# Where eight stage 1 groups stand among the taps of a long convolution, and which engine empties their tiles

## The chip, the cores and the metric

The kernel runs on one core of one Trainium2 chip. The metric is the device time in microseconds of one execution; the time of a kernel is the median over its runs. A profile is one execution recorded instruction by instruction, and its span is counted from the first to the last recorded instruction.

## The reference, cut to what matters

```
k_shift[t, d] = sum over j of k[t - j, d] * shift_k[d, j]        # ks = 4
kv   = k_shift * v                                                # S = 2048, D = 512
y    = irfft2( rfft2(pad kv to 2S) * rfft2(pad ssm_k to 2S) )[:S] + kv * ssm_D
h    = x + layernorm(x) * y                                       # x = A_q
out  = h + relu(layernorm(h) @ w1) @ w2                           # w1 512 x 1376
```

Everything is bf16 at the edges. The convolution is along the 2048 tokens, one filter (a row of `ssm_k`) for each of the 512 channels.

## The kernel before, in words

The long convolution is done as a two-step Fourier transform with matmuls. Both operands, the filter `ssm_k` and the product `kv`, go through the same three steps: `to_rows` transposes them with TensorE into a flat layout (`kfl` for the filter, `xfl` for kv), `stage1` does the short first transform, and `stage2` the second one. After the filter's spectrum and the signal's spectrum are multiplied, two inverse steps and a two-layer MLP follow.

**What loads.** SyncE issues nine loads in the order of line 119: chunk 0 of k, the whole of `ssm_k`, chunk 0 of v, and then chunks 1, 2 and 3 of k and of v in turn. A chunk is 512 tokens. The k and v chunks are DMA transposes (lines 125 and 127), so that channels come to lie on partitions: `kT` holds k, `vTs[c]` holds chunk c of v.

**The taps.** `taps(u)` (line 271) makes one of 16 units. `u` is split into a chunk `c = u // 4` and a block of 128 channels `rg = u % 4`. Four matmuls of 128x128 by 512 columns accumulate the four shifted products in one PSUM tile `pkv` (line 275). `times_v(u, ps)` (line 282) multiplies that tile by `vTs[c]` on VectorE and writes it to `kvx`. Units 0 to 3 run before the transposes of the filter. Units 4 to 15 run inside the loop of line 311.

**The stage 1 groups.** `group_k(gb)` (line 286) is group gb of eight for the filter. It takes four PSUM tiles, and for each of 8 columns and two halves of the table it issues four small matmuls (a load of 32x128 weights and a matmul with 64 columns, line 248): 64 pairs of load and matmul, 128 instructions, in about 0.6 us. Then each of the four tiles is copied into `a1k` by ScalarE or VectorE: the string given to `stage1` has one letter a tile, A for ScalarE (`copy`, line 235) and D for VectorE (line 237), read by `engs[(4 * gb + rg) % len(engs)]`.

**What sets the order.** The schedule is written by hand: every engine runs its instructions in the order of the program text. All PSUM tiles of this part have one tag (`ps`) in a pool of 8 banks; a new tile takes the bank that was given back longest ago, and its first matmul waits for the copy that empties this bank.

**What comes after.** `to_rows` for kv (line 321) transposes `kvx` in eight steps of 8 transposes (line 221, tiles `pst`), each emptied by VectorE (line 225) or ScalarE (line 230). The first of its transposes reads all channels and all chunks, so it waits for the last `times_v` (u = 15). Then `spectrum_k` (stage 2 of the filter, lines 263, 265, 335 and 336) alternates with the stage 1 groups of kv, which have the same line 248 but read `xfl`.

I number the filter's groups gk0 to gk7 and the units u4 to u15. In the kernel before, TensorE's order in the loop is: u4 u5 gk0, u6 gk1, u7 u8 gk2, u9 gk3, u10 u11 gk4, u12 gk5, u13 u14 gk6, u15 gk7. Each group's tiles go A, A, D, A.

Of the kernel before, what the change touches and what calls it, by code (L numbers as in the profile page):

```python
# [56 lines left out]
def kernel(  # L57
# [175 lines left out]
    def copy(eng, o, i):  # L233
        if eng == "A":
            nc.scalar.copy(out=o, in_=i)  # L235
        else:
            nc.vector.tensor_copy(out=o, in_=i)  # L237


    def stage1(gb, fl, a_out, engs, parts=1):  # L240
        n = 8 // parts
        for h in range(parts):
            pss = [psum.tile([P, n, 64], F32, tag="ps", name=f"ps1_{r}") for r in range(4)]
            for gi in range(n):
                for f, first in ((f1hi, True), (f1lo, False)):
                    for rg in range(4):
                        rows = slice(32 * rg, 32 * rg + 32)
                        nc.tensor.matmul(out=pss[rg][:, gi, :],  # L248
                                         lhsT=fl[rows, (8 * gb + n * h + gi) // 2, :, :, gi % 2].rearrange("p d n -> p (d n)"),
                                         rhs=f[rows, :], start=first, stop=not first, tile_position=(32 * rg, 0))  # L250
            for rg in range(4):
                copy(engs[(4 * gb + rg) % len(engs)], a_out(gb, 8 * rg + n * h, n),
                     pss[rg][:].rearrange("p g c -> p c g"))
# [17 lines left out]
    def taps(u):  # L271
        c, rg = divmod(u, DC)
        ps = psum.tile([P, CH], F32, tag="ps", name="pkv")
        for j in range(KS):
            nc.tensor.matmul(out=ps[:], lhsT=wdiag[:, rg, j, :], rhs=kT[:, rg, CH * c + 16 - j:CH * c + CH + 16 - j],  # L275
                             start=(j == 0), stop=(j == KS - 1))
        return u, ps

    def times_v(u, ps):
        c, rg = divmod(u, DC)  # L280
        split = "p (a h l) -> p a h l"
        nc.vector.tensor_tensor(out=kvx[:, :, rg, 8 * c:8 * c + 8, :].rearrange("p h a l -> p a h l"),  # L282
                                in0=ps[:].rearrange(split, h=16, l=4),
                                in1=vTs[c][:, rg, :].rearrange(split, h=16, l=4), op=ALU.mult)

    def group_k(gb):
        stage1(gb, kfl, lambda o, j, n: a1k[:, :, 32 * o + j:32 * o + j + n], "AADAAADA")

    first = [taps(u) for u in range(4)]
    warm_up(7)  # L290
# [1 line left out]
    kfl = early.tile([P, 32, 2, 64, 2], BF16, name="kfl")  # L292
# [15 lines left out]
    a1k = a1[:, 8 * 256:72 * 256].rearrange("p (c j) -> p c j", j=256)  # L308
    a1x = a1[:, 0:64 * 256].rearrange("p (o c j) -> p o c j", o=8, j=32)

    for gb in range(8):
        for u in ((4, 5), (6,), (7, 8), (9,), (10, 11), (12,), (13, 14), (15,))[gb]:
            times_v(*taps(u))
        group_k(gb)
    for pq in halves:
# [364 lines left out]
```

## Time and profile before

| what | value |
|---|---|
| median of 13 runs | 219.98 us (218.8 to 220.74) |
| the profiled execution's own time | 219.25 us |
| its span | 217.5 us |
| TensorE busy | 205.7 us, 95% of the span |
| VectorE busy | 147.4 us, 68% |
| ScalarE busy | 128.1 us, 59% |
| the loop of lines 311 to 314 on TensorE | 18.51 us (u4 starts) to 37.03 us (first transpose of kv) |
| matmul line 275, 128x512 | 380 ns each by the record, four in about 0.93 us |
| VectorE multiply by v, line 282 | 680 to 693 ns |
| VectorE copy of a stage 1 tile, line 237 | 686 ns |
| ScalarE copy of a stage 1 tile, line 235 | 595 ns |

How to read it: the span is some 1.75 us shorter than the execution's time, which has a start and an end around it. Durations of neighbours on one engine overlap a little: three ScalarE copies in a row take 1.56 us, six take 3.16 us, and VectorE starts a new tile every 0.60 us while each record is 0.69 us long. In the rows of the profile, "<-" behind an idle time names what ended it, and "issue" means that nothing which the profile shows was waited for. PEld is the loading of weights, which has its own row beside PE.

### The profile page before, as it was taken

What the parts mean: (1) busy time and instruction counts of PE and PEld (TensorE: products, weight loads), DVE (VectorE), ACT (ScalarE), POOL (GpSimd) and SP (SyncE); (2) the same over time, 40 slices, a digit from 0 to 9 for tenths busy, and PEclk for the clock granted to TensorE, in tenths of its full rate; (3) what the DMA queues carried; (4) which work ended last, traced back from release to release, by engine and by line L of the source; (5) the groups of instructions that cost most, each with busy time, mean ns of one, the idle gap of its engine ahead of it and who ended that gap; (6) DMA issues with size and microseconds to landing.
All of it is one profiled execution on the core that took longest, in us unless ns stands there. A gap on an engine that the chain in (4) does not pass through costs nothing.

```text
span 217.5 us, 7309 instructions
## 1 busy us (share of the span) xinstructions
PE 205.7 (95%) x3129; PEld 140.0 (64%) x3129; DVE 147.4 (68%) x303; ACT 128.1 (59%) x241; POOL 65.5 (30%) x99
## 2 busy tenths in 40 slices
PE   7979889999999999999987999999999999999993
PEld 2466446999989999889955687444444444444442
DVE  6977678899989998958967778743874267130032
ACT  2487857788878888868865699004740067106500
POOL 6049930000039999968000121210021002000000
PEclk9999999999999999999999799999999999999999
DMA  6999960000000000069960000422123110531012
GB/s 136 360 187 176 193 127 8 3 5 3 3 3 3 2 3 0 0 161 215 323 214 6 3 3 0 60 60 55 27 57 68 33 44 0 85 75 36 0 42 54
DMA packets 30383, 15.40 MB, mean 71 GB/s; under 512 B 25520, under 2 KB 29072, under 8 KB 30224
## 3 DMA queue, kind: packets, MB, share of 16 engines
q1 hardware_dynamic: 28992, 14.75, 29.8%
q8 instruction: 24, 0.39, 0.7%
q10 hardware_dynamic: 1360, 0.20, 0.6%
q14 instruction: 7, 0.06, 0.1%
HBM read 7.08 MB, written 2.10 MB: 42 GB/s over the span
## 4 chain that ended last, share of the span: by engine, by line
PE 77%; SPq 9%; DVE 6%; DMA 3%; ACT 2%; issue 2%; DVEq 0%
PE ps2m L595 18%; PE ps1m L583 16%; PE pz L509 10%; PE psy L385 7%; SPq L127 5%; PE psi L454 4%; PE ps2k L263 4%; PE u L263 4%; PE ps L248 4%; PE u L265 4%; SPq L125 3%; PE ps2k L265 3%; DMA vT<-in_A_v_dram 3%; PE pkv L275 3%; DVE bp L237 2%
## 5 line engine op out<-in xcount | busy, mean ns | idle before, releaser
L585 ACT ACTIVATE h1T<-ps1m 128x512 bf16<-128x512 f32 (+3 forms) x55 | 27.4, 514 | 21.2 <-PE ps1m L583 20.3
L583 PE MATMUL ps1m<-hlnT,w 128*128 128x512 bf16 (+3 forms) x220 | 39.6, 336 | 0.3
L595 PE MATMUL ps2m<-w,h1T 128*128 128x512 bf16 (+3 forms) x187 | 39.8, 367 | 0.0
L597 DVE TENSOR_TENSOR o<-ps2m,xh 128x512 bf16<-128x512 f32 (+1 forms) x17 | 11.1, 659 | 38.1 <-PE ps2m L595 37.6
L583 PEld LDWEIGHTS <-w 128*128 128x128 bf16 (+1 forms) x220 | 21.8, 100 | 17.6 <-issue 1.4
L595 PEld LDWEIGHTS <-h1T 128*128 128x128 bf16 (+1 forms) x187 | 17.6, 98 | 21.2 <-issue 3.1
L509 PE MATMUL pz<-bp,ecore 32*32 32x128 f32 x1024 | 23.2, 386 | 2.9 <-issue 2.3
L520 ACT CAST zt<-pz 128x512 bf16<-128x512 f32 x16 | 8.4, 593 | 29.5 <-PE pz L509 28.2
L235 ACT CAST a<-ps 128x512 fp32r<-128x512 f32 x40 | 21.1, 593 | 4.3 <-PE ps L248 4.3
L529 POOL TENSOR_SCALAR rstd<-mv 128x4 f32<-128x4 f32 (+1 forms) x7 | 1.6, 232 | 70.5 <-DVE mv L536 70.5
L509 PEld LDWEIGHTS pz<-bp,ecore 32*32 32x32 f32 x1024 | 14.4, 106 | 10.4 <-issue 6.8
L375 POOL TENSOR_TENSOR t<-usb,kf 128x320 fp32r<-128x320 f32 x22 | 19.5, 914 | 1.7 <-ACT usb L366 1.6
L375 DVE TENSOR_TENSOR t<-u,kf 128x704 fp32r<-128x704 f32 x22 | 18.5, 899 | 1.7 <-ACT usb L366 1.6
L235 ACT CAST kf<-psy 128x512 fp32r<-128x512 f32 x30 | 17.6, 644 | 1.8 <-PE psy L385 0.3
L534 DVE BATCH_NORM_STATS2 st<-xh 128x6 f32<-128x512 bf16 x28 | 17.4, 681 | 0.0
L237 DVE CAST a<-ps 128x512 fp32r<-128x512 f32 x24 | 15.8, 686 | 1.9 <-PE ps L248 1.9
L275 PE MATMUL pkv<-kT,wdiag 128*128 128x512 bf16 x64 | 15.6, 384 | 0.0
L454 PE MATMUL psi<-dre,kf 128*128 128x256 f32 x64 | 15.2, 284 | 0.2 <-ACT kf L235 0.2
L454 PE MATMUL psi<-dim,kf 128*128 128x256 f32 x64 | 15.1, 285 | 0.0
L213 POOL TENSOR_SCALAR c2n<-c2s 128x512 fp32r<-128x512 f32 x8 | 11.9, 1509 | 9.1 <-ACT c2s L181 9.1
L282 DVE TENSOR_TENSOR kvx<-pkv,vT 128x512 bf16<-128x512 f32 x16 | 10.7, 688 | 4.6 <-DMA vT<-in_A_v_dram 2.6
L336 ACT CAST kf<-ps2k 128x512 fp32r<-128x512 f32 x16 | 10.7, 666 | 3.1 <-PE ps2k L265 1.8
(123 smaller groups left out, 402.4 us busy)
## 6 DMA issues: line engine op xcount, KB each, us to landing
pre<-in_A_ssm_k_dram SPq DMA_DIRECT2D x1, 2048.0 KB, 10.5
out_dram<-o SPq DMA_DIRECT2D x58, 32.0 KB, 1.6
xh<-in_A_q_dram SPq DMA_DIRECT2D x4, 384.0 KB, 7.0
w<-in_B_w_dram SPq DMA_DIRECT2D x1, 1376.0 KB, 12.4
w<-in_B_w_dram SPq DMA_DIRECT2D x1, 1280.0 KB, 15.4
xh<-in_A_q_dram SPq DMA_DIRECT2D x4, 128.0 KB, 3.3
hlnT<-hln SPq DMA_TRANSPOSE x12, 2.4
w<-in_B_w_dram SPq DMA_DIRECT2D x1, 96.0 KB, 15.1
```

Of the source, the lines that this page charges most:

```text
L235: nc.scalar.copy(out=o, in_=i)
L237: nc.vector.tensor_copy(out=o, in_=i)
L263: nc.tensor.matmul(out=ps[:, kk, :], lhsT=w_re[:, k1, :], rhs=a_in(col(k1, 0)), start=True, stop=False, skip_group_check=True)
L265: nc.tensor.matmul(out=ps[:, kk, :], lhsT=w_im[:, k1, :], rhs=a_in(col(k1, 1)), start=False, stop=True, skip_group_check=True)
L275: nc.tensor.matmul(out=ps[:], lhsT=wdiag[:, rg, j, :], rhs=kT[:, rg, CH * c + 16 - j:CH * c + CH + 16 - j], start=(j == 0), stop=(j == KS ...
L375: eng.tensor_tensor(out=t[:, :, j, :], in0=in0.unsqueeze(1).to_broadcast([P, 2, n, 2]), in1=kfr[:, :, j, ks], op=ALU.mult)
L454: nc.tensor.matmul(out=ps, lhsT=kf[:, c, 4 * m:4 * m + 4, :].rearrange("p r k -> p (r k)"), rhs=(dre, dim)[c][:].rearrange("p a b -> p (a ...
L509: nc.tensor.matmul(out=pz[32 * a:32 * a + 32, r4, l4, :], lhsT=ecore[rows, rho, n2, :], rhs=rhs, start=(rho == 0), stop=(rho == 1), tile_p ...
L534: nc.vector.bn_stats(out=st[:, t % 4, :], in_=xh[:, t, :])
L583: nc.tensor.matmul(out=ps1[:fsz, :], lhsT=w1[:, c, fc * P:fc * P + fsz], rhs=hlnTs[sc][:, c, part], start=(c == 0), stop=(c == DC - 1))
L585: nc.scalar.activation(out=h1s[sc][:fsz, fc, part], in_=ps1[:fsz, :], func=ACT.Relu)
L595: nc.tensor.matmul(out=ps2[:], lhsT=h1s[sc][:ksz, fc, i * P:(i + 1) * P], rhs=w2[:ksz, fc, ds], start=(fc == 0), stop=(fc == NFC - 1))
```

## The change

Two lines change. The units of the taps are handed out differently over the eight groups, and the string of engines is written out for all 32 tiles.

```diff
     def group_k(gb):
-        stage1(gb, kfl, lambda o, j, n: a1k[:, :, 32 * o + j:32 * o + j + n], "AADAAADA")
+        stage1(gb, kfl, lambda o, j, n: a1k[:, :, 32 * o + j:32 * o + j + n], "AADAADADADADADADADADADADAAAAAAAA")
...
     for gb in range(8):
-        for u in ((4, 5), (6,), (7, 8), (9,), (10, 11), (12,), (13, 14), (15,))[gb]:
+        for u in ((4, 5), (6, 7), (), (), (8, 9), (10, 11), (12, 13), (14, 15))[gb]:
             times_v(*taps(u))
         group_k(gb)
```

TensorE's order in the loop becomes: u4 u5 gk0, u6 u7 gk1, gk2, gk3, u8 u9 gk4, u10 u11 gk5, u12 u13 gk6, u14 u15 gk7. So gk0 to gk3 stand ahead of u8, the first unit of the third chunk, and gk1, gk2 and gk3 stand in a row. The tiles go A, A, D, A in gk0, A, D, A, D in gk1 to gk5, and A, A, A, A in gk6 and gk7: VectorE has 11 of the 32 copies (8 before) and ScalarE 21 (24 before). TensorE's instructions are the same in number and kind. GpSimd's and SyncE's instructions and their order are unchanged.

## The prediction

> **What bounds the kernel now.** I read the page first, then the chain of waits, and then TensorE's and VectorE's timelines cut to 18 to 43 us, because both edits lie inside the loop that ends at 37.03 us.
>
> ```profile
> PE 205.7 (95%) x3129; PEld 140.0 (64%) x3129; DVE 147.4 (68%) x303; ACT 128.1 (59%) x241; POOL 65.5 (30%) x99
> ```
>
> TensorE is busy for 95% of the span, so what moves the time is mainly where it stands still. The chain of waits, cut to the loop (start, length, what):
>
> ```profile
> 20.76 5.71 DMA vT<-in_A_v_dram
> ...
> 26.56 0.70 DVE kvx L282
> ...
> 27.30 0.67 PE ps L248 x62
> 27.97 1.84 PE pkv L275 x8
> ...
> 31.39 0.31 PE ps L248 x25
> 31.70 0.65 issue
> 32.35 0.47 PE ps L248 x39
> ```
>
> Two stops stand in it. Up to 27.30 gk3 waited for a bank that u8 still held, and u8's multiply waited for v's chunk 2, which landed at about 26.5. At 31.70 TensorE stopped in gk5 after 25 of its 64 pairs, and nothing that the profile shows was waited for. A third, of 0.51 us up to 22.56, is gk1 waiting for the bank of u5. From 32.35 the chain is TensorE's own work, then u15's multiply at 36.28, and the first transpose at 37.03.
>
> What is the stop at 31.70? The page has a queue that carries code, and the weight loads show stops of the same kind later:
>
> ```profile
> q8 instruction: 24, 0.39, 0.7%
> ```
> ```profile
> 32.34 0.37 PEld L248 LDWEIGHTS <-kfl 32*128 32x128 bf16 x39 [0.77 <-issue]
> ...
> 114.69 2.29 PEld L509 LDWEIGHTS pz<-bp,ecore 32*32 32x32 f32 x127 [1.32 <-issue]
> 118.30 2.37 PEld L509 LDWEIGHTS pz<-bp,ecore 32*32 32x32 f32 x128 [1.33 <-issue]
> 121.66 0.21 PEld L509 LDWEIGHTS pz<-bp,ecore 32*32 32x32 f32 x10 [0.98 <-issue]
> ```
>
> 24 packets of 0.39 MB are 16 KB each. Between the last three stops TensorE ran 127 and 128 load-and-matmul pairs, some 256 instructions: one packet is one block of 256. The DMA view cut to 119 to 121 us, and then to 29 to 31 us, places the packet in time (40 slices of 0.05 us, GB/s; in the second the row falls off as the transposes end and jumps as the packet starts):
>
> ```profile
> GB/s 0 0 0 0 0 0 0 0 328 0 0 0 0 0 0 0 0 0 0 0 0 0 0 0 0 0 0 0 0 0 0 0 0 0 0 0 0 0 0 0
> ```
> ```profile
> GB/s 287 287 292 287 302 282 292 287 297 287 292 287 292 292 282 307 231 53 36 353 15 20 5 0 0 0 0 0 0 0 0 0 0 0 0 0 0 0 0 0
> ```
>
> On an idle DMA a packet starts 1.1 us after the block before it was entered (118.30 to 119.40), and TensorE goes on 2.26 us later (121.66): one block costs 3.4 us from request to use, and is asked for only when the block before it is entered. Before the stop at 32.34, the packet started at 29.95, though its block's predecessor was entered at about 27.65: it waited for the burst of v's chunk 3 to end. The same view of 24 to 26 us has the packet before that start at 24.35, again as a burst (v's chunk 2) faded; its 3.8% of 16 engines for 2 us is a length of 1.22 us. The one at 29.95 has 3.0%, 0.96 us, and TensorE went on 1.4 us behind its end; the one at 119.40, 3.0% too, 1.3 us.
>
> **The change, part by part.** (1) *The order.* Count the blocks back by 128 pairs from the stop (pair 26 of gk5). Before, blocks begin after pair 37 of gk3 and pair 49 of gk1. After, gk5 has one unit less ahead of it, so blocks begin after pair 29 of gk5, pair 45 of gk3 and pair 45 of gk1. Between the last two lie gk2 and most of gk3 with no taps: 128 pairs at 0.62 us a group, where before 12 matmuls of 0.23 us stood between.
>
> First without any fetch. u4 and u5 are unchanged; u6 and u7 end on TensorE at 22.8. VectorE, from v's chunk 1 on and 0.60 us a tile: u4 21.22, u5 21.83, gk0's tile 22.43, u6 23.03, u7 23.63, two of gk1 from 24.23, two of gk2 from 25.43. gk1 needs the bank of gk0's VectorE tile (23.1), so it runs 23.15 to 23.75. gk2 needs u7's bank (24.3): to 24.95. gk3 needs gk1's last VectorE copy (25.45): it starts at 25.55 and is at pair 45 at 25.95. From there TensorE is not held again: 0.2 us for the rest of gk3, then four times two units and a group (1.84 + 0.62), with u15's taps ending in the fourth. So u15's multiply starts 0.20 + 3 x 2.46 + 1.94 = 9.5 us after pair 45 (the 1.94 is two units until their last multiply starts, by u15's 1.07 before), ends 0.69 later, and the first transpose follows 0.06 later: 10.25 us in all. 25.95 + 10.25 = 36.2, against 37.03: a gain of 0.85 us. v's chunk 3 (32.2) no longer counts, since u12's multiply starts at about 33.
>
> Now the fetch. The block that begins at pair 46 of gk3 is asked for when TensorE reaches pair 45 of gk1, at 23.5. Before, the packet for the block behind gk1 started at 24.35, in the lull after v's chunk 2, took 1.22 us, and TensorE can go on 1.3 to 1.4 us behind a packet's end. So the block is there at 26.95 if the packet starts at 24.35, and at 27.2 if it starts 1.1 us after 23.5. The worst delay seen from request to use (27.65 to 32.34, 4.7 us) gives 28.2. I take 27.1, by the first two rows. Then the first transpose is at 27.1 + 10.25 = 37.35: **a loss of 0.3 us**, the gain of 0.85 less a new stop of 1.15.
>
> The next block (pair 30 of gk5) is asked for at 27.1. TensorE wants it at 27.1 + 0.2 + 2.46 + 1.84 + 0.3 = 31.9. With 3.5 us it is there at 30.6, no stop. If its packet waits behind the burst of v's chunk 3 until 29.95, as the same packet did before, it comes at 32.34, and the stop is 0.45 to 0.55. The request reaches the queue at about 28.2, between the bursts of k's and v's chunk 3, where the traffic dips. Bounds 0 and 0.55; I take 0.2, nearer to the dip. The block after it is asked for with the DMA idle, more than 4 us ahead of need: nothing.
>
> (2) *The engines.* VectorE gets three tiles more, 3 x 0.60 us, all in gk1 to gk5; ScalarE gets three fewer. In my walk VectorE sets gk1's, gk2's and gk3's starts up to 25.95; after that the fetch covers it, and in the tail it is done with gk5's tiles at 33.6 at the latest, before u12 needs it. If that cover were gone (no fetch), it is already in the 36.2. (3) *gk6 and gk7 on ScalarE alone.* VectorE is free at u15's end, so its first copy of the transposes starts at about 0.6 us after the first transpose instead of 0.68. ScalarE's last copy of gk7 ends at about 39.4 instead of 38.49, and its two copies of the transposes (38.60 and 39.94 before) at 40.4 and 41.5; the bank or data that TensorE needs from them is wanted at 42.5 at the earliest. The stage behind runs at TensorE's pace (VectorE waits about 0.24 us for it in each of its turns), so both come to 0, with 0.1 us either way. Everything behind 37.03 shifts as one piece.
>
> Sum: +0.3 + 0.2 + 0 = **+0.5 us**, on the profiled execution 219.25 to 219.75. That execution lies 0.73 below the median of the 13 runs, so I put the same difference on the median: 219.98 + 0.5 = 220.5 us. What a measurement of this kernel can tell from no change is about 0.3%, 0.66 us; the forecast stands just inside.
>
> **A rule that bears on it.** The row is the one above: 256 instructions a packet, and a stop when the next is late. [...]
>
> **The rivals.** *Faster: the fetch stays hidden.* Speaks for it: before, this block was never late, and the stops were of VectorE's making. Against: the stops that ended at 32.34 and 121.66 did so 1.3 to 1.4 us behind a packet, so a packet that starts at 24.35 allows 26.9 at best. It decides if TensorE goes on before 26.8; each us earlier is a us gained, down to -0.85: 219.1 us. Chance 0.14. *Slower by more: the packet falls into the next burst.* The burst of k's chunk 3 starts at 26.2; a request that misses the lull waits like the one before 32.34, and goes on at 28.2 or later: 28.2 + 10.25 = 38.45, +1.4, or 221.4 us. Chance 0.10. *The two cancel*, by a fetch some tenths earlier and no second stop: within 0.2 us of before, 220.0 us. Chance 0.06. *VectorE as the bound* would need its backlog to reach u12 behind 34.0; the walk has 33.6. It is inside the forecast's range.
>
> **How the numbers follow.** The forecast (a new stop in gk3, with the second stop from 0 to 0.55) has 0.70 and spans +0.2 to +0.95: 220.2 to 220.95; about half of it lies over +0.66. Slower: half of 0.70, the 0.10 and some of the noise, 0.47. Faster: 0.15. Same: 0.38. The range leaves out the full gain and the far end of the late packet (0.17) and takes in the runs' own scatter of a few tenths: 219.6 to 221.3.
>
> **What would show it.** Right: in the weight loads, gk1 whole at 23.15, gk2 at 24.35, and gk3 cut after 45 pairs with a stop by "issue" that ends at about 27.1; u8's taps at 27.3; the first transpose at 37.3 to 37.9; no wait for v's chunk 3. Wrong: gk3 in one piece ending by 26.2 and the transposes at 36.2 (fetch hidden); the cut at another pair (blocks counted wrongly); a stop that ends by a VectorE copy; or a changed distance from the first transpose to the end of the span, 217.5 - 37.03 = 180.5 us.

## The result, and the profile after

| | before | after |
|---|---|---|
| median | 220.08 us (48 runs, 218.44 to 222.4) | 223.06 us (11 runs, 221.85 to 224.68) |
| profiled execution | 219.25 us, span 217.5 | 222.85 us, span 221.0 |
| mean granted clock of that execution | 0.992 | 0.969 |
| first transpose of kv | 37.03 us | 38.68 us |

The ratio is 1.0144, with a 95% interval of 1.0116 to 1.0172: the change costs about 3.1 us. The forecast had 220.5 us, up to 221.3. Every ratio here leaves out executions more than 1.5% above the fastest of their kernel; the medians keep them.

The page of the profile after, the row of engines and the granted clock over 40 slices of 5.5 us:

```profile
PE 208.3 (94%) x3129; PEld 141.6 (64%) x3129; DVE 148.8 (67%) x306; ACT 126.9 (57%) x238; POOL 65.5 (30%) x99
```
```profile
PEclk9999979999999999999997589999999999999999
```

TensorE runs the same 3129 matmuls, and is busy for 2.6 us more (before: 205.7). More busy time for the same work means slower work, and the second row says where: the granted clock falls in the slice around 30 us, in the loop, and around 120 to 130 us. A matmul at half clock counts as "busy" for longer (the taps' records: 630 ns at the median from 27.6 to 30.1 us, where the granted clock is 0.50, and 380 ns from 31 us on); the busy row alone wouldn't have told this from more work.

The chain of waits after, cut to the loop (start, length, what):

```profile
25.27 0.50 PE ps L248 x42
25.76 1.08 issue
26.85 0.45 PE ps L248 x18
27.30 3.24 PE pkv L275 x8
30.54 0.61 PE ps L248 x64
31.16 1.84 PE pkv L275 x8
...
38.68 3.77 PE pst L221 x64
```

Both the foreseen and the unforeseen stand here. At 25.76 TensorE stops inside gk3 by "issue" for 1.08 us, as forecast. The 8 matmuls of u8 and u9 then take 3.24 us, and the 8 of u10 and u11, the same instructions, 1.84. Most of the first eight run at half speed.

The weight loads after (start, length, engine, line, what, idle time ahead):

```profile
24.07 0.85 PEld L248 LDWEIGHTS <-kfl 32*128 32x128 bf16 x64 [0.51 <-issue]
25.27 0.38 PEld L248 LDWEIGHTS <-kfl 32*128 32x128 bf16 x41 [0.35 <-issue]
26.84 0.29 PEld L248 LDWEIGHTS <-kfl 32*128 32x128 bf16 x19 [1.19 <-issue]
27.23 0.13 PEld L275 LDWEIGHTS <-wdiag 128*128 128x128 bf16 x2
27.63 0.15 PEld L275 LDWEIGHTS <-wdiag 128*128 128x128 bf16 x1 [0.28 <-issue]
...
38.68 3.61 PEld L221 LDWEIGHTS <-kvx 128*128 128x128 bf16 x64 [0.28 <-DVE kvx L282]
```

gk3's first four pairs are the end of the row of 64, so the cut comes after 4 + 41 = 45 pairs. From 27.63 on the loads of the taps come one by one, 0.43 us apart (before, and in every later row of taps, eight loads lie within 1.41 us).

The windows view says why (window, length, busy time and instructions of PE, PEld, DVE, ACT and POOL, then the granted clock, DMA share, GB/s):

```profile
26.00:27.00 1.00, 0.15 (x12) 0.16 (x16) 0.41 (x1) 0.00 (x0) 1.00 (x4) 0.85 1.03 233
27.00:28.00 1.00, 1.00 (x21) 0.42 (x14) 0.67 (x2) 0.70 (x2) 0.94 (x4) 0.50 1.11 252
28.00:29.00 1.00, 1.00 (x4) 0.38 (x3) 0.62 (x2) 0.37 (x1) 0.87 (x3) 0.50 1.25 148
29.00:30.00 1.00, 1.00 (x4) 0.36 (x3) 0.69 (x1) 0.00 (x0) 0.37 (x1) 0.50 1.34 277
30.00:31.00 1.00, 1.00 (x66) 0.53 (x64) 0.42 (x1) 0.00 (x0) 0.00 (x0) 0.94 0.31 24
```

The clock is 0.50 from 26.71 to 30.12 us, 3.41 us long. All but the last 0.42 us of the taps of u8 and u9 (27.30 to 30.54) falls into it: 3.24 - 1.84 = 1.40 us. The 3.4 us ahead of it, in the kernel after, and then the same stretch in the kernel before:

```profile
23.30:26.70 3.40, 1.79 (x137) 1.36 (x124) 3.11 (x6) 2.15 (x4) 3.40 (x6) 1.00 1.29 164
```
```profile
23.30:26.70 3.40, 3.40 (x78) 1.57 (x77) 1.76 (x4) 2.54 (x6) 3.40 (x6) 1.00 1.10 164
```

Before, TensorE was busy throughout, with units of taps between the groups. After, it was busy for 1.79 us of 3.40, and only with the groups' 64-column matmuls.

### The profile page after: what moved, and what is told of

It is laid out like the page before. It is cut to its first block, busy times and chain, and to the rows that moved or that the text cites. A ratio compares the mean times of both kernels' runs of the same rounds, so it can differ in the third digit from the quotient of the medians.

```text
span 221.0 us, 7308 instructions
## 1 busy us (share of the span) xinstructions
PE 208.3 (94%) x3129; PEld 141.6 (64%) x3129; DVE 148.8 (67%) x306; ACT 126.9 (57%) x238; POOL 65.5 (30%) x99
## 4 chain that ended last, share of the span: by engine, by line
PE 78%; DVE 7%; SPq 6%; DMA 3%; issue 3%; ACT 2%; DVEq 0%
PE ps2m L595 18%; PE ps1m L583 16%; PE pz L509 10%; PE psy L385 7%; SPq L127 4%; PE pkv L275 4%; PE psi L454 4%; PE ps2k L263 4%; PE u L263 4%; PE u L265 3%; PE ps L248 3%; PE ps2k L265 3%; DMA vT<-in_A_v_dram 3%; DVE a L237 2%; DVE bp L237 2%
## 5 line engine op out<-in xcount | busy, mean ns | idle before, releaser
L583 PE MATMUL ps1m<-hlnT,w 128*128 128x512 bf16 (+3 forms) x220 | 40.3, 342 | 0.2
L585 ACT ACTIVATE h1T<-ps1m 128x512 bf16<-128x512 f32 (+3 forms) x55 | 27.6, 513 | 21.6 <-PE ps1m L583 20.7
L583 PEld LDWEIGHTS <-w 128*128 128x128 bf16 (+1 forms) x220 | 22.3, 102 | 17.8 <-issue 1.2
L235 ACT CAST a<-ps 128x512 fp32r<-128x512 f32 x37 | 19.7, 593 | 8.0 <-PE ps L248 8.0
L237 DVE CAST a<-ps 128x512 fp32r<-128x512 f32 x27 | 17.3, 685 | 2.8 <-PE ps L248 2.8
L275 PE MATMUL pkv<-kT,wdiag 128*128 128x512 bf16 x64 | 16.5, 407 | 0.0
L454 PEld LDWEIGHTS psi<-dre,kf 128*128 128x128 f32 x64 | 12.1, 192 | 0.7 <-ACT kf L235 0.7
```

The lines of the kernel that those rows point to most:

```text
L454: nc.tensor.matmul(out=ps, lhsT=kf[:, c, 4 * m:4 * m + 4, :].rearrange("p r k -> p (r k)"), rhs=(dre, dim)[c][:].rearrange("p a b -> p (a ...
L583: nc.tensor.matmul(out=ps1[:fsz, :], lhsT=w1[:, c, fc * P:fc * P + fsz], rhs=hlnTs[sc][:, c, part], start=(c == 0), stop=(c == DC - 1))
L585: nc.scalar.activation(out=h1s[sc][:fsz, fc, part], in_=ps1[:fsz, :], func=ACT.Relu)
```

## The experiments

Three questions were open. Is the loss in the order or in the string? Is it all in the loop, or does the clock at 118 to 129 us (three windows of half clock in the profile after, one in the profile before) belong to the change? And within the loop, how much is the fetch and how much the clock? Medians of the kernel before lay between 219.9 and 220.3 us in all the comparisons; each ratio is against the runs beside it.

**The order alone** (`e1_order_only`): the units of after, the string "AADAAADA" of before.

> The order of the changed kernel with the engine string of before (A, A, D, A in every group). Theory (code fetch, then clock): the three groups in a row reach their block of code before it has come, whoever empties the tiles, so gk3 is cut after 45 pairs, the stop ends at 26.8 to 27.2 us, and the granted clock is 0.5 for 3.4 us right behind it; the first transpose of kv stands at 38.5 to 39.0 us, and the time is 222.5 to 223.5. Rival (the emptying of the tiles by VectorE makes the stop): no cut inside gk3, no half clock before 30 us, first transpose at 36.2 to 37.4, time at most 220.5.

Measured: 223.52 us, ratio 1.0136 [1.0089, 1.0183]. The order carries the loss, as expected of the time. The cut, the stop and the clock that were expected stay unseen for this kernel: its one profiled execution took 660.99 us and can't stand for the others.

**The string alone** (`e2_string_only`): the units of before, the string of 32 letters.

> The order of before with the engine string of the changed kernel (more copies on VectorE in gk1 to gk5, gk6 and gk7 on ScalarE alone). Theory: the string costs nothing by itself; first transpose of kv at 36.8 to 37.4 us, no half clock before 40 us, time 219.5 to 220.5, as before. Rival (the string carries part of the loss): first transpose at 37.6 or later, or a half clock window before 40 us, and time over 221.

Measured: 220.83 us, 1.0017 [0.9984, 1.0049]; first transpose 37.21. The median lies 0.3 us over the expected range and under the rival's 221; the string costs nothing that can be told from the scatter. Its weight loads also test the count of blocks, which put a boundary after pair 37 of gk3 in the order of before:

```profile
26.97 0.35 PEld L248 LDWEIGHTS <-kfl 32*128 32x128 bf16 x37 [0.43 <-issue]
27.69 0.26 PEld L248 LDWEIGHTS <-kfl 32*128 32x128 bf16 x27 [0.38 <-issue]
```

The cut is there, with a stop of 0.38 us behind a packet that started at 25.35. In the order of before this block is only just in time, or just late.

**The stretch filled with work** (`e3_fill_gk3`): eight 128x512 matmuls into gk3's own tile ahead of its pairs, whose result is overwritten.

```diff
+            for _ in range(idle):     # idle = 8 in gk3
+                nc.tensor.matmul(out=pss[0][:].rearrange("p g c -> p (g c)"), lhsT=wz[:, 0:P], rhs=wz[:], start=True, stop=True)
```

> The changed kernel with 8 matmuls of 128x128 by 512 columns, whose result is overwritten, ahead of gk3: they fill the time in which TensorE stands still for its code (8 x 0.216 = 1.7 us from 24.9 on). Theory (the idle time, not the fetch, is what lowers the clock): no half clock between 26 and 31 us, taps at 0.23 us a matmul again, first transpose of kv at 37.2 to 37.6 instead of 38.68, so about 1.3 us of the 3.1 come back: 221.5 to 222.0. If the loss between 110 and 130 us is caused by the first one, all but 0.3 comes back: 220.2 to 220.6. Rival (the clock falls because three groups of small matmuls stand in a row, whatever stands beside them): half clock as in the changed kernel, and the 1.7 us of filling come on top of the stop or hide in it: 223 or more.

Measured: 221.59 us, 1.0057 [1.0021, 1.0093]: 1.84 us of added work on TensorE, and by the medians the kernel is 1.5 us *faster* than without; the interval lies wholly under that of the change (1.0116 to 1.0172). The profiled execution is one of the longer ones, 224.05 us. The weight loads (two lines further down in this kernel) and the windows:

```profile
27.00 0.35 PEld L250 LDWEIGHTS <-kfl 32*128 32x128 bf16 x37 [0.42 <-issue]
29.89 0.26 PEld L250 LDWEIGHTS <-kfl 32*128 32x128 bf16 x27 [2.54 <-issue]
30.20 1.41 PEld L277 LDWEIGHTS <-wdiag 128*128 128x128 bf16 x8
```
```profile
28.00:29.00 1.00, 0.00 (x0) 0.00 (x0) 0.00 (x0) 0.00 (x0) 0.88 (x3) 1.00 0.19 9
...
30.00:31.00 1.00, 1.00 (x31) 0.56 (x27) 0.64 (x2) 0.68 (x2) 0.00 (x0) 1.00 0.72 161
```

Eight pairs more ahead of gk3's move the cut from 45 pairs to 37, which is the count of blocks once more. The packet came late here, at 27.48, and TensorE stood still from 27.35 to 29.89. So the first transpose, at 40.25, missed the expected 37.2 to 37.6 in this execution. Yet the clock stayed at 1.00 and the taps ran in 1.41 us of loads. So standing still for 2.5 us doesn't by itself halve the clock.

**The loop made longer, nothing else** (`e4_shift_1700ns`): before, with the same eight matmuls ahead of gk7.

> The kernel before with the same 8 matmuls ahead of gk7, where TensorE waits for nothing: everything behind is 1.5 to 1.7 us later and nothing else changes. Theory A (the loss between 110 and 130 us in the changed kernel is chance of the execution, in which windows of the clock fall on the stops): time of before plus 1.6, 221.5 to 221.8, with as many half clock windows as before. Theory B (it follows from everything being later): 223 or more, with two or three half clock windows between 115 and 130 us.

Measured: 221.95 us, 1.0059 [1.0024, 1.0095], +1.3 by the ratio. The weight loads:

```profile
36.09 1.61 PEld L245 LDWEIGHTS <-wz 128*128 128x128 bf16 x8
38.12 0.58 PEld L250 LDWEIGHTS <-kfl 32*128 32x128 bf16 x64 [0.42 <-issue]
38.74 2.32 PEld L221 LDWEIGHTS <-kvx 128*128 128x128 bf16 x41
```

The first transpose moves by 1.71 us, to where the profile after had it (38.68), and the time by no more than that. A later start of the stages behind isn't punished, though this profile too had three windows of half clock (118.62 to 128.86). They come and go: from the mean clocks of 29 runs of before (a window of half clock, 3.413 us at 0.50 from 119.16 on in the profile before, takes 3.413 / 2 = 1.707 us of full clock from a run) there were between 0 and 4 in a run, 1.65 on the mean, and a run was longer by some 0.55 us for each.

**The stretch of line 509 kept busy** (`e5_before_pz_busy`, `e6_after_pz_busy`): one fp32 matmul of 128x128 by 192 into an unused part of `pz` ahead of each quarter of its loop, in before and in after.

```diff
+            if len(l4s) == 2:
+                free = pz[:, 3, 2:4, :] if l4s[0] == 0 else pz[:, 3, 0:2, :]
+                nc.tensor.matmul(out=free.rearrange("p l m -> p (l m)")[:, 0:192], lhsT=bpx[:, 0:P], rhs=bpx[:, 0:192],
+                                 start=True, stop=True, skip_group_check=True)
```

> The kernel before with one more f32 matmul of 128x128 by 192 columns, whose result is not used, ahead of each quarter of the first two inverse steps (line 509), where TensorE stands still for code for about 1.2 us in each block of 128 pairs. Theory (the half clock windows between 115 and 130 us come from low matmul activity in that stretch, and their number, 0 to 4 an execution, is most of the scatter of the runs of before): fewer half clock windows than before's mean of 1.65 (0.5 or less), a scatter of the runs below 2 us, and a time from 0.8 us faster to 0.4 us slower than before, by how much of the filling hides in the stops. Rival (the windows have another cause): as many windows as before, time of before plus 0 to 2.5 us.

> The changed kernel with the same eight matmuls. With the stretch from 115 to 130 us out of the way, what is left between this kernel and the kernel before with the same matmuls is the loop alone. Theory (all of the loss arises in the loop: a stop for code of 0.3 to 3 us, by whether the packet catches the lull between the transposes, and taps at half clock): the difference of the two stays near 3 us. Rival (half of the loss is that the stretch behind sees more half clock windows): the difference is 1.6 to 1.9 us.

Measured: 220.82 us, 1.0038 [1.0017, 1.0059], and 223.52 us, 1.0124 [1.0074, 1.0174]. The windows of 120 to 125 us, of before, of after and of before with the filling:

```profile
120.00:125.00 5.00, 4.46 (x148) 2.86 (x120) 3.83 (x11) 3.06 (x6) 0.96 (x2) 0.74 0.01 3
```
```profile
120.00:125.00 5.00, 3.72 (x141) 2.64 (x141) 3.81 (x11) 3.51 (x5) 0.96 (x2) 0.50 0.02 3
```
```profile
120.00:125.00 5.00, 5.00 (x166) 2.95 (x142) 3.83 (x12) 3.60 (x6) 0.96 (x2) 1.00 0.03 7
```

The filling keeps the clock up there (0.28 windows in a run by the mean clocks) and narrows the scatter of before to 1.2 us, but costs 0.8 us itself, where at most 0.4 was expected. With the clock's chance at 110 to 130 us mostly gone, the change still costs 2.7 us by the medians, or 0.0086 x 220 = 1.9 by the ratios. The second figure is the one that the rival had forecast, and the intervals are too wide for the times to decide. The two profiled executions show more: neither has half clock behind the loop, the first transposes are 40.81 - 37.18 = 3.63 us apart, and what follows takes 182.0 us in e6 and 182.5 in e5.

**A lighter filling** (`e10_before_pz_light`): two bf16 matmuls of 128x128 by 256 in place of the fp32 one.

> The kernel before with two bf16 matmuls of 128x128 by 256 columns (0.107 us each at full clock) ahead of each quarter of the first two inverse steps, a lighter filling than the f32 one, which cost 0.8 us. Theory (half clock windows between 115 and 130 us cost before 0.4 to 0.6 us each, 1.5 an execution): if this is enough activity, 0.5 windows or fewer and a time 0.2 to 0.7 below before, 219.4 to 219.9; if not, as many windows as before and 0.2 to 0.6 above it.

Measured: 219.96 us, 0.9997 [0.9958, 1.0035], with 0.51 windows in a run where the runs beside it had 1.75. At full clock, bf16 matmuls of 256 columns start 0.109 us apart in the profile before (line 583), beside the expected 0.107. The clock can be held, but the 0.2 to 0.7 us that were expected to be won don't show; the interval reaches from 0.9 us won to 0.8 lost.

**The changed kernel again** (`a2_changed_again` to `a5_changed_again`): four single executions with a profile each.

> The changed kernel, unaltered, profiled a second time, to see how much of its loop varies. Theory: gk3 is cut after 45 pairs again. If the packet of code catches the lull behind v's chunk 2, the stop ends at 26.8 to 27.2 us and the first transpose stands at 37.3 (full clock) to 38.7 (half clock for 3.4 us); if it misses it, as in the execution of the kernel with the filling, the stop ends near 29.9 and the first transpose stands at 40 to 41.5. Rival: the cut is at another place or absent.

> The same a third time: the same two cases. If all three profiles have the early packet, the share of executions that miss the lull is small and the rest of the loss lies behind the loop.

> The changed kernel profiled again, for the share of late packets: early (gk3 goes on by 27.2, first transpose at 38.5 to 39.0) or late (28.5 to 30, first transpose at 40 to 41.5), by whether the packet's request, 1.1 us behind pair 45 of gk1, comes before or after the end of the burst of v's chunk 2.

> The same once more: an early or a late packet, by the same rule of request against burst, with the first transpose at 38.5 to 39.0 or at 40 to 41.5.

Measured, with the first profile ahead:

| execution | time | packet starts | gk3 goes on | windows of half clock in the loop | first transpose |
|---|---|---|---|---|---|
| after | 222.85 | 24.47 | 26.84 | 26.71 to 30.12 | 38.68 |
| a2 | 221.0 | 24.75 | 27.09 | 27.76 to 31.17 | 38.96 |
| a3 | 223.74 | 26.28 | 28.71 | 26.62 to 33.45 | 41.14 |
| a4 | 222.01 | 25.55 | 28.11 | 26.49 to 33.32 | 40.72 |
| a5 | 225.53 | 25.54 | 28.45 | 26.52 to 33.35 | 40.93 |

So there are two cases, and the first profile had shown the milder. The weight loads of a3, and the DMA view of 24 to 28 us (40 slices of 0.1 us, GB/s) of after and of a3:

```profile
25.98 0.38 PEld L248 LDWEIGHTS <-kfl 32*128 32x128 bf16 x41 [0.35 <-issue]
28.71 0.29 PEld L248 LDWEIGHTS <-kfl 32*128 32x128 bf16 x19 [2.34 <-issue]
```
```profile
GB/s 287 257 202 182 364 230 195 169 51 31 8 13 10 20 13 8 10 8 10 10 10 15 276 292 289 289 287 292 287 289 294 292 292 289 289 201 192 200 223 243
```
```profile
GB/s 287 287 289 292 289 294 289 292 282 254 251 261 269 179 87 46 5 5 38 79 215 287 443 279 269 269 269 74 18 10 0 0 0 0 5 10 8 8 10 10
```

In after the transposes fade at 24.2, the packet starts (364 GB/s, in the fifth slice), and the next burst comes at 26.2. In a3 the transposes hold 250 to 290 GB/s past 25.2, and the packet's peak (443) comes at 26.2, in the midst of the next rise. TensorE then goes on at 28.71, and a second window of half clock follows the first.

**Chunk 3 left out** (`e7_before_no_chunk3`, `e8_changed_no_chunk3`, `e9_changed_no_chunk3_fill`): the loads of chunk 3 of k and v are left out of before, of after, and of after with the filling of e3, and GpSimd sets that part to zero; the last quarter of the taps works on zeros. No burst then follows v's chunk 2.

```diff
-    for c, src in ((0, "k"), (0, "s"), (0, "v"), (1, "k"), (1, "v"), (2, "k"), (2, "v"), (3, "k"), (3, "v")):
+    for c, src in ((0, "k"), (0, "s"), (0, "v"), (1, "k"), (1, "v"), (2, "k"), (2, "v")):
...
+    nc.gpsimd.memset(kT[:, :, 16 + 3 * CH:16 + 4 * CH], 0.0)
+    nc.gpsimd.memset(vTs[3][:], 0.0)
```

> The kernel before with the loads of chunk 3 of k and of v left out (those parts hold zeros). With fewer bursts the code for gk5 comes at once: the stop in gk5 goes, the first transpose of kv stands at 36.0 to 36.5 us, time 0.5 to 1.0 below before: 219.2 to 219.6. No half clock before 100 us.

> The changed kernel without the same two loads. Theory (whether the packet for gk3 goes out before or behind the next burst of a transpose is what divides the executions of the changed kernel): no burst follows v's chunk 2, every execution has the early packet, gk3 is cut after 45 pairs and goes on at 26.7 to 27.2, and only the half clock remains (in a window without taps): first transpose at 38.4 to 38.9, time 1.9 to 2.5 above the kernel before without chunk 3, scatter smaller than in the changed kernel, no execution with a stop to 28.7 or later. Rival (the late packet has another cause): stops to 28.7 or later as before, and 3 us or more above.

> The same with the 8 filling matmuls ahead of gk3. Theory: the early packet in every execution and no half clock window before 100 us, taps at 0.23 us a matmul; first transpose at 36.9 to 37.4, time 0.7 to 1.1 above the kernel before without chunk 3, and 1.2 to 1.5 below the changed kernel without chunk 3: that difference is the price of the half clock on the taps. Rival (the half clock does not depend on the filling): no difference, or slower.

Measured: e7 219.03 us, 0.9951 [0.9917, 0.9985]; e8 222.53 us, 1.0101 [1.004, 1.0163]; e9 221.39 us, 1.0052 [1.0016, 1.0088]. The weight loads of e7 around gk5, which stopped for 0.77 us before:

```profile
30.72 0.58 PEld L250 LDWEIGHTS <-kfl 32*128 32x128 bf16 x64 [0.42 <-issue]
```

gk5 is whole: the stop of before was a packet behind v's chunk 3, as the prediction read it. The first transpose of e7 is at 35.62. Then e8 and e9:

```profile
27.24 0.20 PEld L250 LDWEIGHTS <-kfl 32*128 32x128 bf16 x19 [1.22 <-issue]
27.52 0.13 PEld L277 LDWEIGHTS <-wdiag 128*128 128x128 bf16 x2
27.93 0.15 PEld L277 LDWEIGHTS <-wdiag 128*128 128x128 bf16 x1 [0.27 <-issue]
```
```profile
26.79 0.35 PEld L252 LDWEIGHTS <-kfl 32*128 32x128 bf16 x37 [0.42 <-issue]
27.32 0.26 PEld L252 LDWEIGHTS <-kfl 32*128 32x128 bf16 x27 [0.18 <-issue]
27.64 1.41 PEld L279 LDWEIGHTS <-wdiag 128*128 128x128 bf16 x8
```

This is the cleanest pair. In both the packet is early and gk3 goes on at 27.24 and 27.32. Without the filling the clock is 0.50 from 27.41 to 30.82 and the first transpose comes at 39.17; with it there is no half clock in the loop and it comes at 37.68. The difference, 1.49 us (1.14 by the medians), is the clock on the taps. Two expectations missed: e8 costs 3.5 us over e7, not 1.9 to 2.5, and e9 2.4, not 0.7 to 1.1. The first transposes differ by as much in e8 (39.17 - 35.62), since e7 was some 0.6 us earlier there than the middle of what was expected and e8 some 0.5 later. So the change loses even where no burst is in the packet's way. (In all three kernels gk0 starts at about 21.0, 0.7 us later than in before, so they are compared with each other.)

**gk0 kept off VectorE** (`e11_gk0_scalar`): after with "AAAA" for gk0, so that VectorE is free earlier and gk1's block may be entered before the lull.

> The changed kernel with gk0's third tile on ScalarE instead of VectorE (string AAAA for gk0): gk1 no longer waits for that copy and enters the block of code behind it some 0.3 us earlier, so the request for gk3's code is earlier against the end of the burst of v's chunk 2. Theory (request before the burst ends: early packet; after it: behind the next burst): the packet starts at 24.2 to 24.8, gk3 goes on at 26.7 to 27.2 in nearly every execution, half clock on the taps remains, time 0.3 to 1.2 below the changed kernel: 221.9 to 222.7. Rival (early and late are drawn by chance whatever the request): time of the changed kernel, 223.0 to 223.4.

Measured: 223.01 us, 1.0113 [1.0072, 1.0154]: the theory missed, and the median is the rival's. Weight loads:

```profile
25.19 0.39 PEld L248 LDWEIGHTS <-kfl 32*128 32x128 bf16 x41 [0.21 <-issue]
28.20 0.29 PEld L248 LDWEIGHTS <-kfl 32*128 32x128 bf16 x19 [2.62 <-issue]
```

The block was entered at 23.24, and the packet still started late, at 25.88.

**One unit put back between** (`e12_one_unit_between`):

```diff
-        for u in ((4, 5), (6, 7), (), (), (8, 9), (10, 11), (12, 13), (14, 15))[gb]:
+        for u in ((4, 5), (6,), (), (7,), (8, 9), (10, 11), (12, 13), (14, 15))[gb]:
```

> The changed kernel with u7 moved from ahead of gk1 to between gk2 and gk3: the same four groups ahead of u8, the same string, no added work. gk1 starts at about 22.6, so the request is as early as before, and the stretch between 23.2 and 26.8 has one unit of taps in it. Theory: early packet, gk3 cut after 45 pairs and going on at 26.7 to 27.1, no half clock or in few executions (0.92 us of dense matmuls in the window), first transpose at 37.1 to 37.5, time 220.3 to 221.2, some 2 to 2.7 below the changed kernel. Rival (three groups' worth of stop lowers the clock whatever the taps): half clock as in the changed kernel, 222 or more.

Measured: 220.50 us, 1.0012 [0.9978, 1.0047], 2.5 us below the changed kernel. Weight loads:

```profile
24.71 0.42 PEld L248 LDWEIGHTS <-kfl 32*128 32x128 bf16 x45 [0.42 <-issue]
26.86 0.20 PEld L248 LDWEIGHTS <-kfl 32*128 32x128 bf16 x19 [1.72 <-issue]
27.11 1.41 PEld L275 LDWEIGHTS <-wdiag 128*128 128x128 bf16 x8
```

gk3 is cut after 45 pairs as in after, the stop is longer (1.72 us) and ends at the same time, 26.86. But u7's four matmuls lie in the stretch, the clock stays at 1.00, and the first transpose comes at 37.75. All four stage 1 groups still stand ahead of u8. Later, gk5 is cut after 29 pairs and stops for 0.43 us, the second stop of the prediction, which puts the first transpose behind the expected 37.1 to 37.5. This version equals the kernel before and doesn't beat it; none that does all the work and was run does.

## Why the prediction was wrong

**Right: the blocks.** gk3 was cut after pair 45, and in e2 and e3 after 37 pairs, where the count of 128 pairs puts it. u12 didn't wait for v's chunk 3. The walk had the groups about 0.3 us too late throughout (gk1's pair 45 came at 23.18, not 23.5). That u8's taps started at 27.30 in the first profile, as said, is luck: the stop ended 0.26 us early, and the rest of gk3 took 0.46 us, partly at half clock, instead of 0.20; in the other four they started between 27.4 and 29.2. The rival in which the fetch stays hidden, down to -0.85, fell: the stop was 0.9 to 2.4 us long in the five profiles of the changed kernel.

**Wrong, the step that failed: "then four times two units and a group (1.84 + 0.62)".** These 10.25 us from gk3's going on to the first transpose are right at full clock: e3 took 40.25 - 29.89 = 10.36 with eight pairs more, e9 37.68 - 27.32 = 10.36. In the five profiles of the changed kernel the distance is 11.84 (26.84 to 38.68), 11.87, 12.43, 12.61 and 12.48, on the mean 12.25. That is 2.0 us more than the sum had. The prediction took the durations of taps and pairs from rows of before, where the clock in the loop was full, and didn't ask whether the change leaves the clock as it is: it took all the dense work out of one stretch of 3.4 us and put three groups of small matmuls and a stop there. The rival with the late packet, 221.4 us, fell short of 223.06 for the same reason: it too had the taps at full clock.

**Wrong, the size of the fetch.** The stop was to end at 27.1 in the likeliest case, and at 28.2 or later if the packet fell into the next burst, which got a chance of 0.10. The first profile (26.84) agrees; but of five, three are of the late kind. The mean is 27.84, 0.74 us more than the sum had. That gk1's block would be asked for some tenths from the end of a burst was on the page; it called for a chance near one half.

**The sum, mended.** The forecast's first transpose was 37.35, against 37.03 in the profile before; the mean of four profiles with the loop of before (before, e2, e5 and e10: 37.03, 37.21, 37.18 and 37.47) is 37.22. So 37.35 - 37.22 = 0.13, and 0.74 for the packet, and 2.00 for the clock: 2.87 us, which is the mean of five after (40.09) less 37.22. Behind the loop nothing is lost on the mean: the five executions' times less their first transposes give 223.03 - 40.09 = 182.94 on the mean, and before 220.08 - 37.22 = 182.86. The five scatter from 181.3 to 184.6, so this mean is good to some 0.6 us. The mean clocks agree with it: the first 12 executions of the changed kernel had 2.9 windows of half clock on the mean, before had 1.65; the five profiles had 1.6 in the loop, which leaves 1.3 of the 2.9 for the rest, no more than before. The 1.85 us that the profile after has on top, with its three windows of half clock near 120 us, belongs to that execution, not to the change; e4 says the same.

**The small terms.** The string and gk6 and gk7 on ScalarE: 0 foreseen, and e2 agrees within its interval. The second stop, in gk5: 0.2 foreseen, none seen in the five. Its packet did start only as the burst of v's chunk 3 ended (at 29.91 in the profile after), so the choice of the dip was wrong, but the slow taps had moved the need behind it. In e12, with the taps at full clock, the same late packet (29.84) gave a stop of 0.43 us, near the bound of 0.55.

**Left open.** What decides between the early and the late packet wasn't controlled. By the traces, a block that was entered up to 23.20 had an early packet in five of five profiles, one that was entered from 23.24 on, with chunk 3 loaded, a late one in eight of nine; in the one exception (a2, 23.62) the burst ended some 0.25 us later than in after. e11 was to move the entry and got no further than 23.24. That a race between the request and the end of v's chunk 2 decides it fits this, but is argued, not shown. Nor is the wait simply one for a quiet DMA: in a3 the DMA was nearly idle from 25.5 to 25.9 (46, 5, 5 and 38 GB/s in the view above), the block had been entered at 23.89, and its packet still started only at 26.28.

## What to carry to other kernels

Before work is moved, look at what stays behind: a stretch that loses its dense matmuls can lose the clock too (here 0.50 for 3.41 us in the profile after), and then the next dense work pays, here 1.4 us for eight matmuls. One unit of 128x512 taps left in the stretch kept the clock, and gave back 2.5 of 3.1 us (e12); even useless dense matmuls paid, 1.5 us by the medians (e3). A run of more than 256 small instructions in less than the 3.4 us that a block of code took to arrive (before, 118.30 to 121.66) stopped in each profile of the changed order in which the loop can be read, by the weight loads for 0.18 us (e9) to 3.15 us (e6). Where the request for the block lands near the end of a DMA burst, one profile shows only one of the two outcomes: take several.

## What the runs showed of the hardware

**The clock follows the kind of work as well as the standing still.** Windows of half clock were 3.41 us long, or twice and three times that, and within a profile they start whole numbers of 3.413 us apart (in the profile after 26.71 and 118.87, 27 windows; in e3 14.33 and 120.14, 31; e12 has one alone, at 217.67). So the full-clock windows between them can be laid out too. Ahead of half clock lay, in the changed kernel, windows with TensorE busy for 1.8 to 2.3 of 3.41 us with (almost) only 64-column matmuls, and in the profile before, 115.75 to 119.16, one busy for 2.54 us with the small fp32 matmuls of line 509. Windows with some 512-column matmuls kept the clock though they were no busier: e12, 23.11 to 26.52, 2.08 us busy, 0.98 of it with taps; e3, 27.98 to 31.39, 1.50 us busy, 1.19 of it with taps, and 1.91 us of the stop. 0.41 us of taps was too little (a2, 24.35 to 27.76, 2.10 us busy). But small matmuls alone didn't always lose it: those of line 509 kept full clock in each window in which they were busy for 2.67 us or more at full clock (a2, 116.50 to 119.92: 2.74), lost it in each at 2.43 or less, and went either way between. So the kind of work and the stop both count; how much of each is enough was not measured finer than this.

**A packet of code comes late beside DMA transposes.** With no burst in the way, or one that was fading, packets started 0.8 to 1.6 us after the block before was entered; in eight other profiles 1.7 to 3.4 us after it (e3: entered 24.06, started 27.48). A running burst doesn't always keep it out: in a3 and a4 the packet started while the next burst ran (26.28 and 25.55), 2.4 and 2.1 us after entry. What held it until then no run here shows.
